# Attention forward: the two score matmuls of a step, each over its own 64 rows of the array

## The chip, the cores and the metric

The kernel runs as one program on one core of a Trainium2 chip. The engines named below are PE (TensorE, the matrix array; PEld is its weight load), DVE (VectorE), ACT (ScalarE), POOL (GpSimd) and SP (SyncE, which issues DMAs). The metric is the device time of one execution in microseconds (us); the median of repeated executions counts, and lower is better.

## The reference, cut to what matters

The whole program is the forward and the backward of one transformer block with modulated layer norms. It returns the block's output and nine gradients. The change lies in the attention of the forward pass, which reads:

```
B, S, D = 1, 2048, 512;  H = 32;  Dh = 16
q, k, v = heads of (h @ wqkv)                     # h: modulated layer norm of x
scores  = einsum('bhqd,bhkd->bhqk', q, k) * Dh ** -0.5
p       = softmax(scores, axis=-1)
o       = einsum('bhqk,bhkd->bhqd', p, v)
out     = o (heads side by side) @ wo
```

All inputs and outputs are bf16. For each of 32 heads there is a 2048 x 2048 matrix of scores, each score a sum over only 16 products, and each must pass through an exponential.

## The kernel before

**Layout.** Heads are kept in 8 groups of 4 (index g). For a group, the keys lie transposed in one tile KTq of 128 partitions by 2048 tokens: head j of the group has rows 32j to 32j+15, and rows 32j+16 to 32j+31 are zeros. Queries are stored in DRAM (QTq_d) in the same way. Four tiles QTm0 to QTm3 of 128 x 512 hold the queries of one head each: QTm[j] has head j in rows 32j to 32j+31 and zeros everywhere else, so that a matmul over all 128 rows of KTq and QTm[j] gives the scores of head j alone, the other heads being multiplied by zero.

**Loops.** The forward attention (`phase_fwd`, L267) runs over `order` (L313): 4 chunks of 512 queries (qc), in each 8 groups (g), in each two head pairs (jp). One such triple is a unit; there are 64. A unit has 16 steps, one for each block of 128 keys (kb), so there are 1024 steps. Before the change the pair jp consists of heads 2jp and 2jp+1 of the group. In a step

1. two score matmuls (L388, a = 0, 1) write 128 keys x 512 queries of each head to the two halves of a PSUM tile `st` (128 x 1024 fp32, two banks; the pool has two such tiles);
2. one ACT instruction (L391) takes the exponential of the whole tile and writes `pu` in bf16 to SBUF;
3. eight small matmuls (L322, in `pv`) of an earlier step multiply `pu` blocks (128 x 128, as weights) by 17 columns of Vaug (16 value columns and a column of ones, which gives the softmax denominator), and accumulate in `accbank`.

At the end of a unit DVE divides by the denominators (L329, L330), and POOL issues DMAs for what the next unit needs: two loads of 32 rows into the QTm tiles (`load_q`, L302), and every second unit a KTq tile (L309).

**Order.** PE and SP run in the order in which the program is written. Into each step the loop mixes background work: `bg` is a generator that first makes the remaining queries and keys (chunk 0, L631), and later runs the MLP and part of its backward for the chunk before (L1187 to L1254, L1296). `bg.step(rate)` takes on average 1.2 (chunk 0) or 1.14 (later) background matmuls of 512 columns for each step; L398 to L404 then put fewer or more of the small L322 matmuls in the step, so that a step with two background matmuls has fewer of them and a later one catches up. The order is fixed when the program is built and does not depend on measured times.

**Opening.** The first two units (32 steps, L348 to L362) are interleaved with the making of the first keys, queries and values (`gen_open`, L426). For them the queries come straight from the projection: `gen_fm` (L624) copies the 32-row strips of heads 0 to 3 into QTo0, QTo1, QTm2 and QTm3 (L641; strip 1 on ACT, the others on DVE). The six tiles QTo and QTm are first filled with zeros on DVE (L465, L469).

After the forward attention come the last chunk's MLP and weight gradients, then the attention backward (`attn_bwd`, L1422), then the last gradients. The change touches none of these. The backward matters here only because its score matmuls (L1568) and its dP matmuls (L1494) already contract over 64 rows, one in each half of the array.

Of the kernel before, what the change touches and what calls it, by code (L numbers as in the profile page):

```python
# [9 lines left out]
BF16 = mybir.dt.bfloat16  # L10
# [9 lines left out]
P = 128  # L20
# [15 lines left out]
class Background:  # L36
# [13 lines left out]
    def next(self):  # L50
        while self.gens:
            r = next(self.gens[0], None)
            if r is not None:
                if isinstance(r, tuple):
                    self.mark = r[0]
                    self.seen.add(r[0])
                return r
            self.gens.pop(0)
        return None
# [46 lines left out]
class K:  # L106
# [160 lines left out]
    def phase_fwd(self):  # L267
# [5 lines left out]
        tc, nc, pp = self.tc, self.nc, self.pp  # L273
# [15 lines left out]
        fw = self.open_pool("fw", bufs=1)  # L289
# [4 lines left out]
        stp = self.open_pool("fwst", bufs=2, space=PSUM)  # L294
        accp = self.open_pool("fwacc", bufs=2, space=PSUM)
        O32 = self.ra.tile([P, 4, D], F32, name="O32")
        QTm = [fw.tile([P, 512], BF16, name=f"QTm{j}") for j in range(4)]

        def load_q(qc, g, jp):
            with tc.high_priority():  # L300
                for j in (2 * jp, 2 * jp + 1):
                    nc.gpsimd.dma_start(QTm[j][32 * j:32 * j + 32, :], self.QTq_d[g, 32 * j:32 * j + 32, 512 * qc:512 * (qc + 1)])  # L302

        def load_k(qc, g):
            if qc == 0:
                return self.KT_next
            t = kp.tile([P, S], BF16, name="KTq")
            with tc.high_priority():
                nc.gpsimd.dma_start(t[:], self.KTq_d[g])  # L309
            return t  # L310
# [7 lines left out]
        def pv(w):  # L318
            (u, a, sub) = w
            (n, qc, g, jp, kb, acc, pu) = u  # L320
            h = 4 * g + 2 * jp + a
            nc.tensor.matmul(acc[:, a, sub, :], lhsT=pu[:, a, sub * P:(sub + 1) * P], rhs=Vaug[:, kb, h, :],  # L322
                             start=(kb == 0 and a == 0 and sub == 0), stop=False, skip_group_check=True)
            if kb < ST - 1 or (a, sub) != (1, 3):
                return
            st0 = 4 * qc
            for a in range(2):
                h = 4 * g + 2 * jp + a
                nc.vector.reciprocal(self.rl[:, st0:st0 + 4, h], acc[:, a, :, DH])  # L329
                nc.vector.tensor_tensor(O32[:, :, h * DH:(h + 1) * DH], acc[:, a, :, 0:DH],  # L330
                                        self.rl[:, st0:st0 + 4, h:h + 1].to_broadcast([P, 4, DH]), ALU.mult)
            if (g, jp) == (NQ - 1, 1) and qc < SC - 1:
                bg.add(self.gen_mlp(qc, self.take_o(qc, O32)))

        KT = kp.tile([P, S], BF16, name="KTq")
# [4 lines left out]
        QTo = []  # L340
# [7 lines left out]
        for i, (n, kb) in enumerate(units):  # L348
            if i == len(units) // 2:
                bg.until(1)  # L350
                load_q(*order[2])
            stt = stp.tile([P, 2, 512], F32, name="st")
            for a in range(2):
                nc.tensor.matmul(stt[:, a, :], lhsT=KT[:, kb * P:(kb + 1) * P], rhs=(QTm[2 + a] if n else QTo[a])[:],
                                 start=True, stop=True)
            pu = pup.tile([P, 2, 512], BF16, name="pu")
            nc.scalar.activation(pu[:], stt[:], ACT.Exp, scale=self.scale)
            u = (n, 0, 0, n, kb, accs[n], pu)
            next(first)
            pend.extend((u, a, sub) for a in range(2) for sub in range(4))  # L360
            while len(pend) > 24:
                pv(pend.pop(0))  # L362
# [5 lines left out]
        KT = self.KT_next  # L368
        for n, (qc, g, jp) in list(enumerate(order))[2:]:
            if (qc, g, jp) == (1, 0, 0):  # L370
                bg.drain()
                es.close()
                self.close_qkv()
                self.open_mlp()
                bg.add(self.gen_weights())
            accb = accp.tile([P, 512], F32, name="accbank")
            acc = accb[:, 0:8 * (DH + 1)].rearrange("p (a s e) -> p a s e", a=2, s=4)
            self.cur_g = g
            for kb in range(ST):
                if kb == (5 if qc == 0 and jp == 1 else 1) and n + 1 < len(order):  # L380
                    if n < 2 * NQ - 1 and jp == 1:
                        bg.until(g + 1)
                    load_q(*order[n + 1])
                    if jp == 1:
                        KTn = load_k(*order[n + 1][:2])
                stt = stp.tile([P, 2, 512], F32, name="st")
                for a in range(2):
                    nc.tensor.matmul(stt[:, a, :], lhsT=KT[:, kb * P:(kb + 1) * P], rhs=QTm[2 * jp + a][:],  # L388
                                     start=True, stop=True)
                pu = pup.tile([P, 2, 512], BF16, name="pu")  # L390
                nc.scalar.activation(pu[:], stt[:], ACT.Exp, scale=self.scale)  # L391
                u = (n, qc, g, jp, kb, acc, pu)
                now = n * ST + kb
                pend.extend((u, a, sub) for a in range(2) for sub in range(4))
                if late:
                    late.pop(0)()
                rate = 1.14 if qc else 1.2
                room = int((SPAN - 2 - bg.plan(rate)) / PVT)  # L398
                while pend:
                    age = now - max(pend[0][0][0] * ST + pend[0][0][4], 2 * ST - 2)  # L400
                    if age < 2 or (room <= 0 and age < 4):
                        break
                    pv(pend.pop(0))
                    room -= 1  # L404
                bg.step(rate)
            if jp == 1 and n + 1 < len(order):
                if n < 2 * NQ - 1:
                    bg.until(-(g + 1))
                KT = KTn
# [9 lines left out]
        while pend:  # L419
            pv(pend.pop(0))  # L420
# [5 lines left out]
    def gen_open(self, Vaug, KT, QTm, QTo, stp, bg):  # L426

        tc, nc, io = self.tc, self.nc, self.io
# [4 lines left out]
        sa_ = self.open_pool("p1a", bufs=1)  # L433
# [30 lines left out]
        nc.gpsimd.memset(Vaug[:, :, :, DH:DH + 1], 1.0)  # L464
        nc.vector.memset(QTm[0][:], 0.0)  # L465
        self.silu_c(ps)
        QTo.extend(sa_.tile([P, 512], BF16, name=f"QTo{j}") for j in range(2))
        for t in QTo + QTm[1:]:
            nc.vector.memset(t[:], 0.0)  # L469
        for t in self.wpad0 + wpads[::-1]:  # L470
# [2 lines left out]
        def warm(n):  # L473
            w = stp.tile([P, 2, 512], F32, name="st")
            for _ in range(n):
                nc.tensor.matmul(w[:, 0, :], lhsT=self.ones_b[:], rhs=QTm[0][:], start=True, stop=True)
# [47 lines left out]
        def pad0(t):  # L524
            nc.scalar.copy(self.wpad0[t][:].rearrange("p k (j e) -> p k j e", e=32)[:, :, :, 0:DH],
                           wq[:, :, t * D:t * D + 4 * DH].rearrange("p k (j d) -> p k j d", d=DH))
# [7 lines left out]
        def fm(*a, **k):  # L534
            for _ in self.gen_fm(ps, *a, **k):
                pass
# [22 lines left out]
        warm(4)  # L559
        fm(1, 0, 0, dst=KT[:, 0:512])  # L560
        pad0(0)
        fm(0, 0, 0, masked=QTo + QTm[2:])
        warm(2)
        for st in range(4, 8):
            stat(st)
# [1359 lines left out]
```

## Time and profile before

| | |
|---|---|
| median of 3 runs | 2545.73 us (2542.11 to 2547.05) |
| the profiled execution | 2545.66 us; its span 2543.9 us, granted TensorE clock 0.996 |
| opening, first to 33rd exponential | 16.7 to 64.2 us |
| the other 992 steps of the forward attention | 64.2 to 979.3 us |
| in that stretch (915.10 us): busy PE, ACT, DVE, POOL | 893.06, 912.01, 277.25, 271.06 us |

The profile is one execution taken by the hardware profiler. A line of its groups gives the source line, the engine, the operation, the tiles written and read, the shapes and the count; then the busy time in us and the mean length of one in ns; then the time for which the engine was idle just before them, and what ended it. For a matmul, `128*128` or `64*128` are the rows and columns of the array that it uses. A matmul's recorded end is modelled and includes the time in the pipeline: the next matmul may begin long before it. So for PE the distance from one start to the next says what an instruction costs, not its recorded length. Lines of the timeline are: start in us, length in us from the first start to the last end, engine, source line, operation, tiles, shape and count.

### The profile page before, as it was taken

How to read it: one execution, taken by the hardware profiler on the slowest of the kernel's cores; microseconds unless marked ns; L12 is line 12 of the kernel's file. 1: busy time of each engine (PE TensorE's matmuls, PEld its weight loads, DVE VectorE, ACT ScalarE, POOL GpSimd, SP SyncE). 2: the span in 40 equal slices, each digit the busy share in tenths (PEclk: the TensorE clock that was granted, in tenths of full speed). 3: DMA queues.
4: the chain of work that ended last, by engine and by line, in shares of the span. 5: the costliest groups of instructions: out<-in, count | busy, mean ns of one | idle time of the engine just before them, and what ended most of it. 6: DMA issues, size and time to landing. Idle time of an engine off the chain costs nothing.

```text
span 2543.9 us, 76653 instructions
## 1 busy us (share of the span) xinstructions
PE 2453.8 (96%) x30727; PEld 1201.3 (47%) x30727; DVE 1700.3 (67%) x3523; ACT 2299.9 (90%) x3757; POOL 707.1 (28%) x1265
## 2 busy tenths in 40 slices
PE   8999899999999999999999999999999999999998
PEld 4555555555555554663444444444444444443443
DVE  6222223423332343677999999999999999999957
ACT  7999999999999997436999999999999999999935
POOL 2454521220231031354222222222222222222223
PEclk9999999999999999999999999999999999999999
DMA  4588652440351053898999999999999999999996
GB/s 165 117 179 197 169 106 80 103 116 23 107 135 49 22 162 102 165 208 197 221 219 216 217 217 218 218 216 213 216 219 217 219 218 214 217 220 233 231 211 175
DMA packets 1258571, 442.07 MB, mean 174 GB/s; under 512 B 1203540, under 2 KB 1227222, under 8 KB 1258214
## 3 DMA queue, kind: packets, MB, share of 16 engines
q1 hardware_dynamic: 1219078, 336.03, 68.1%
q0 software_dynamic: 37056, 100.11, 13.2%
q8 instruction: 240, 3.93, 0.6%
q10 hardware_dynamic: 2080, 1.05, 0.1%
q14 instruction: 117, 0.96, 0.1%
HBM read 73.73 MB, written 62.40 MB: 54 GB/s over the span
## 4 chain that ended last, share of the span: by engine, by line
PE 58%; ACT 26%; DMA 8%; issue 5%; DVE 2%; POOL 1%; SPq 0%; DVEq 0%; ACTq 0%; POOLq 0%
ACT pu L391 18%; PE st L1568 15%; PE st L388 8%; PE acckv L1448 8%; PE accq L1470 7%; DMA dsT<-ds 7%; ACT pu L1571 6%; PE accbank L322 3%; PE dp L1494 2%; PE dps L1047 2%; PE pps L1234 2%; PE dp L1618 1%; PE pps L631 1%; PE dps L992 1%; PE st L1713 1%
## 5 line engine op out<-in xcount | busy, mean ns | idle before, releaser
L1498 DVE TENSOR_TENSOR ds<-dp,pu 128x512 bf16<-128x512 f32 x1920 | 1169.9, 681 | 67.9 <-PE dp L1494 46.6
L1571 ACT ACTIVATE pu<-st 128x512 bf16<-128x512 f32 x2048 | 1075.8, 626 | 49.1 <-PE st L1568 21.3
L391 ACT ACTIVATE pu<-st 128x1024 bf16<-128x1024 f32 x992 | 912.0, 1077 | 3.1 <-PE st L388 2.9
L388 PE MATMUL st<-QTm,KTq 128*128 128x512 bf16 x1984 | 587.7, 377 | 19.5 <-ACT pu L391 6.0
L322 PEld LDWEIGHTS <-pu 128*128 128x128 bf16 x8192 | 347.6, 96 | 235.7 <-issue 2.3
L322 PE MATMUL accbank<-Vaug,pu 128*128 128x17 bf16 x8192 | 357.7, 171 | 1.2 <-ACT Vaug L522 0.9
L1470 PEld LDWEIGHTS <-dsT 128*128 128x128 bf16 x8192 | 240.1, 96 | 229.4 <-issue 199.8
L1494 PE MATMUL dp<-m,q 64*128 64x512 bf16 x1024 | 344.4, 382 | 1.6 <-DVE g2w L1053 0.7
L1494 PE MATMUL dp<-m,dOTg 64*128 64x512 bf16 x1024 | 344.2, 382 | 0.1
L1568 PE MATMUL st<-m,QTg 64*128 64x512 bf16 x1024 | 322.1, 381 | 12.2 <-ACT pu L1571 7.5
L1568 PE MATMUL st<-m,q 64*128 64x512 bf16 x1024 | 321.6, 382 | 11.3 <-ACT pu L1571 6.7
L388 PEld LDWEIGHTS <-KTq 128*128 128x128 bf16 x1984 | 187.9, 96 | 176.1 <-issue 124.5
L1507 POOL TENSOR_TENSOR ds<-junk,pu 128x512 bf16<-128x512 f32 x64 | 74.1, 1157 | 412.6 <-ACT junk L1506 412.6
L302 POOL DMA_DIRECT2D QTm<-QTq_d x124 | 63.1, 511 | 341.0 <-PE st L388 319.5
L1448 PE MATMUL acckv<-ds,Qg 128*16 128x512 bf16 x1024 | 154.5, 382 | 0.0
L1448 PE MATMUL acckv<-pu,dOg 128*16 128x512 bf16 x1024 | 154.4, 382 | 0.0
L1448 PE MATMUL acckv<-pu,q 128*16 128x512 bf16 x1024 | 154.0, 381 | 0.0
L1448 PE MATMUL acckv<-ds,q 128*16 128x512 bf16 x1024 | 154.0, 381 | 0.0
L1470 PE MATMUL accq<-Kg,dsT 128*128 128x16 bf16 x4096 | 143.7, 170 | 10.3 <-DMA dsT<-ds 9.9
L1507 POOL TENSOR_TENSOR ds<-csq,pu 128x512 bf16<-128x512 f32 x64 | 73.9, 1154 | 281.5 <-ACT csq L1506 281.5
L1470 PE MATMUL accq<-q,dsT 128*128 128x16 bf16 x4096 | 144.6, 170 | 3.8 <-DMA dsT<-ds 3.6
L329 DVE RECIPROCAL rl<-accbank 128x4 f32<-128x4 f32 x128 | 22.9, 179 | 159.6 <-PE accbank L322 159.4
(383 smaller groups left out, 2980.3 us busy)
## 6 DMA issues: line engine op xcount, KB each, us to landing
KTq<-KTq_d POOLq DMA_DIRECT2D x24, 512.0 KB, 4.0
duT_d<-auT POOLq DMA_DIRECT2D x3, 1792.0 KB, 7.9
aT_d<-rT POOLq DMA_DIRECT2D x3, 1792.0 KB, 11.3
KTq_d<-KTq SPq DMA_DIRECT2D x32, 128.0 KB, 1.8
QTq_d<-ev_fm SPq DMA_DIRECT2D x32, 128.0 KB, 3.9
VTq_d<-vT POOLq DMA_DIRECT2D x4, 1024.0 KB, 6.5
dsT<-ds SPq DMA_TRANSPOSE x256, 7.2
dx<-dx_d SPq DMA_DIRECT2D x16, 256.0 KB, 5.6
```

The source lines that it names most:

```text
L302: nc.gpsimd.dma_start(QTm[j][32 * j:32 * j + 32, :], self.QTq_d[g, 32 * j:32 * j + 32, 512 * qc:512 * (qc + 1)])
L322: nc.tensor.matmul(acc[:, a, sub, :], lhsT=pu[:, a, sub * P:(sub + 1) * P], rhs=Vaug[:, kb, h, :], start=(kb == 0 and a == 0 and sub == 0) ...
L388: nc.tensor.matmul(stt[:, a, :], lhsT=KT[:, kb * P:(kb + 1) * P], rhs=QTm[2 * jp + a][:], start=True, stop=True)
L391: nc.scalar.activation(pu[:], stt[:], ACT.Exp, scale=self.scale)
L1047: nc.tensor.matmul(pt[:], lhsT=a[st], rhs=g_tm[:, st, :], start=(st == 0), stop=(st == ST - 1))
L1448: nc.tensor.matmul(acckv[r:r + DH, :], lhsT=T[n][:, ib, col:col + DH], rhs=src[:, a, :], start=(ib == 0), stop=(ib == ST - 1))
L1470: nc.tensor.matmul(accq[:, ib, a, :], lhsT=dsT[:, (i * 2 + a) * 4 + sub, :], rhs=T["K"][:, 4 * c + sub, col:col + DH], start=(c == 0 and i ...
L1494: nc.tensor.matmul(dp[:], lhsT=T["dOT"][rd, ib * P:(ib + 1) * P], rhs=masked["VT"][2 * jp + a][rd, 512 * c:512 * (c + 1)], start=True, sto ...
L1498: nc.vector.tensor_tensor(dsg[:, i, a], dp[:], pu[:, a, :], ALU.mult)
L1507: nc.gpsimd.tensor_tensor(dsg[:, i, 1], f[:], pu[:, 1, :], ALU.mult)
L1568: nc.tensor.matmul(stt[:], lhsT=T["QT"][rs, q], rhs=masked["KT"][2 * jp + a][rs, c0:c0 + 512], start=True, stop=True)
L1571: nc.scalar.activation(pu[:, a, :], stt[:], ACT.Exp, scale=self.scale)
```

## The change

The two heads of a unit are now heads jp and jp+2 of the group, which lie in different 64-row halves of KTq (head j in rows 32j to 32j+31). The two heads of a unit share one tile: QTm[jp] holds head jp in the lower half and head jp+2 in the upper half, each with zeros in the other 32 rows of its half. Each of the two score matmuls reads rows 0 to 63 or rows 64 to 127 of KTq and of QTm[jp]. The four tiles QTm become two and the two QTo become one, so that three of the zero fills on DVE are no longer issued; the copies and loads of strips remain as many as they were, with other targets. PE, ACT, POOL and SP issue the same instructions in the same order as before.

```
-        QTm = [fw.tile([P, 512], BF16, name=f"QTm{j}") for j in range(4)]
+        QTm = [fw.tile([P, 512], BF16, name=f"QTm{j}") for j in range(2)]
...
-                for j in (2 * jp, 2 * jp + 1):
-                    nc.gpsimd.dma_start(QTm[j][32 * j:32 * j + 32, :], self.QTq_d[g, 32 * j:32 * j + 32, 512 * qc:512 * (qc + 1)])
+                for j in (jp, jp + 2):
+                    nc.gpsimd.dma_start(QTm[jp][32 * j:32 * j + 32, :], self.QTq_d[g, 32 * j:32 * j + 32, 512 * qc:512 * (qc + 1)])
...
-            h = 4 * g + 2 * jp + a
+            h = 4 * g + jp + 2 * a
...
             for a in range(2):
-                nc.tensor.matmul(stt[:, a, :], lhsT=KT[:, kb * P:(kb + 1) * P], rhs=(QTm[2 + a] if n else QTo[a])[:],
+                r = slice(64 * a, 64 * a + 64)
+                nc.tensor.matmul(stt[:, a, :], lhsT=KT[r, kb * P:(kb + 1) * P], rhs=(QTm[1] if n else QTo[0])[r, :],
                                  start=True, stop=True)
...
                 for a in range(2):
-                    nc.tensor.matmul(stt[:, a, :], lhsT=KT[:, kb * P:(kb + 1) * P], rhs=QTm[2 * jp + a][:],
-                                     start=True, stop=True)
+                    r = slice(64 * a, 64 * a + 64)
+                    nc.tensor.matmul(stt[:, a, :], lhsT=KT[r, kb * P:(kb + 1) * P], rhs=QTm[jp][r, :], start=True, stop=True)
...
-        QTo.extend(sa_.tile([P, 512], BF16, name=f"QTo{j}") for j in range(2))
+        QTo.append(sa_.tile([P, 512], BF16, name="QTo"))
...
-        fm(0, 0, 0, masked=QTo + QTm[2:])
+        fm(0, 0, 0, masked=[QTo[0], QTm[1]] * 2)
```

## The prediction, made before the changed kernel ran

> **What bounds the kernel now.** First the page: the span, the engines' shares, the chain that ended last, and the groups of the forward attention.
>
> ```profile
> span 2543.9 us, 76653 instructions
> ...
> PE 2453.8 (96%) x30727; PEld 1201.3 (47%) x30727; DVE 1700.3 (67%) x3523; ACT 2299.9 (90%) x3757; POOL 707.1 (28%) x1265
> ...
> ACT pu L391 18%; PE st L1568 15%; PE st L388 8%; PE acckv L1448 8%; PE accq L1470 7%; DMA dsT<-ds 7%; ACT pu L1571 6%; PE accbank L322 3%; PE dp L1494 2%; PE dps L1047 2%; PE pps L1234 2%; PE dp L1618 1%; PE pps L631 1%; PE dps L992 1%; PE st L1713 1%
> ...
> L391 ACT ACTIVATE pu<-st 128x1024 bf16<-128x1024 f32 x992 | 912.0, 1077 | 3.1 <-PE st L388 2.9
> L388 PE MATMUL st<-QTm,KTq 128*128 128x512 bf16 x1984 | 587.7, 377 | 19.5 <-ACT pu L391 6.0
> ```
>
> PE and ACT both look full, and ACT sits idle for 3.1 us before its 992 exponentials, so at first sight nothing is to be had from PE. But the chain runs through both: exponentials (18%) and score matmuls (8%) in turn. So I went to the steady stretch in the busy times by window, and there to the starts of single instructions in the timeline.
>
> ```profile
> 64.20:979.30 915.10, 893.06 (x11003) 500.55 (x11000) 277.25 (x805) 912.01 (x993) 271.06 (x465) 1.00 0.46 111
> ```
>
> The 992 steps take 915.1 us, 922 ns each. PE in the timeline at 700 us:
>
> ```profile
> 700.37 0.38 PE L1296 MATMUL pps<-wogaT,dxT 128*128 128x512 bf16 x1
> ...
> 700.63 0.59 PE L388 MATMUL st<-QTm,KTq 128*128 128x512 bf16 x2
> ...
> 701.06 0.37 PE L322 MATMUL accbank<-Vaug,pu 128*128 128x17 bf16 x9
> ...
> 701.29 0.38 PE L1234 MATMUL pps<-W1mT,auT 128*128 128x512 bf16 x1
> ```
>
> Two score matmuls hold PE for 0.43 us (2 x 215 ns from start to start), the small ones 25 ns each, a background matmul 215 ns. But from the one at 700.37 to the next score matmul it is 0.26 us: PE waited some 45 ns, for ACT. From all starts in the trace, a step in this state is a loop over two steps, since `st` has two buffers: an exponential is recorded for 1088 ns; 51 ns after its end the first score matmul of two steps later starts; 215 ns later the second; that one is recorded for 377 ns; 101 ns after its end the exponential on it starts. 1088 + 51 + 215 + 377 + 101 = 1832 ns for two steps, 916 for one. Of the 991 distances between starts of these exponentials 747 are 914 to 922 ns: **the latency of this loop sets the step, neither engine's work**. ACT's own pace is the smallest distance, 904 ns; 182 are there, in runs of up to six after each delay, as the loop catches up. The exponentials overlap, so ACT shows no idle time.
>
> **The change part by part.**
>
> *Scores side by side.* What two 64-row matmuls in different halves cost is in the backward of the same trace, PE alone:
>
> ```profile
> 1701.82 0.38 PE L1568 MATMUL st<-m,QTg 64*128 64x512 bf16 x1
> 1701.82 0.38 PE L1494 MATMUL dp<-m,dOTg 64*128 64x512 bf16 x1
> 1702.13 0.56 PE L1470 MATMUL accq<-Kg,dsT 128*128 128x16 bf16 x16
> 1702.62 0.39 PE L1568 MATMUL st<-m,QTg 64*128 64x512 bf16 x1
> ...
> 1703.73 0.38 PE L1448 MATMUL acckv<-pu,dOg 128*16 128x512 bf16 x2
> 1704.04 0.39 PE L1568 MATMUL st<-m,QTg 64*128 64x512 bf16 x1
> ```
>
> The pair starts together (median 4 ns apart over 1792 pairs) and each is recorded for some 385 ns. But each change of the row count costs: from the pair to the first 128-row L1470 it is 305 ns (median of 452), 90 over the 215 of the stream; from a 512-column L1448 to the pair 311 ns (422), 96 over; from the last 16-column L1470 to the pair 101 ns (339), 76 over 25. The forward enters the pair once a step and leaves it once.
>
> Loop: 1088 + 51 + 4 + 385 + 101 = 1629, with the 96 of entry behind the wait 1725, both under 2 x 904 = 1808. So ACT's own pace takes over, with 83 to 179 ns of slack for each two steps.
>
> PE: the pair held it for 430 ns; now 4 + 305 + 96 = 405. The other matmuls of a step are 353 ns in the mean (counted at 25 and 215 ns), 455 in the heaviest 64 steps (those from 64 us on), plus 17 ns for their own waits; the remaining 122 are PE's wait for ACT (430 + 353 + 17 + 122 = 922). After: 405 + 353 + 17 = 775 in the mean, 867 in the heaviest stretch, both under 904. So PE gains only 25 ns a step; what counts is the 211 ns taken off the loop.
>
> What is late next is ACT alone: 991 x 904 = 895.9 us against 913.1 measured for these distances (the sum is over 904 by some 18 in all, first to last). By kind: the 747 at 914 to 922 and the few up to 930 give 9.9 us, all gone. 29 at 930 to 1000 are over by 1.6: steps with two background matmuls, which the slack now covers. 23 over 1000 are over by 6.6: with 179 ns of each covered (1808 - 1629) 3.7 go and 2.9 stay, most of it one step at 317 us (2.78 us) that waits for a transposing DMA. 9.9 + 1.6 + 3.7 = **15.2 us.**
>
> *Opening.* The 32 steps to 64.2 us take 47.5 us. About twenty are paced by PE (1.5 us: four 512-column matmuls, the small ones, two scores): 25 ns each, with a little where ACT waits on a pair, 0.6 us; 0.1 to 1.6 possible, since in other steps the pair's latency counts.
>
> *Three fills fewer.* They are 0.27 us each and stand ahead of the first statistics on DVE:
>
> ```profile
> 5.29 0.82 DVE L469 MEMSET QTm<- 128x256 uint32 x3
> 6.03 1.22 DVE L486 BATCH_NORM_STATS2 stats<-rT 128x6 f32<-128x512 bf16 x2
> ```
>
> The input that the statistics read landed at 5.08 us, so they move up by 0.8. The chain behind (rstd on POOL, normalization, transposes at 11.18, first score at 16.0) follows until the transposes meet their own predecessors on PE, free at 10.47: 0.7 us. At nothing if the second weight load comes late.
>
> *Copies and loads.* Same number, same places. The first pair now needs two DVE copies (end 16.26 by their lengths) where it needed one and an ACT copy (16.28): nothing. Loads into QTm are issued by POOL with the same predecessors; a tile is written while the other unit's is read, and over ten steps (9 us) remain: nothing. POOL's 319 us of waiting before them is for the score matmuls of the unit before and delays nobody. No wait is added elsewhere; one on PE changes from ACT to DVE in the opening.
>
> *After the forward* nothing changes and the background is counted in steps, so the gain stays. Its DMAs get 18 ns a step less of cover: ten steps, 0.2 us a wait, a few waits: under 1 us, not counted and inside the range.
>
> Sum: 15.2 + 0.6 + 0.7 = 16.5 us. 2545.66 - 16.5 = **2529.2 us**. The profiled execution is 0.07 us from the median of the runs shown, so the same number stands for it.
>
> [...] The 90 and 96 ns above are what this trace charges for a change of row count. [...]
>
> **Rivals.**
>
> *ACT doesn't hold 904.* The runs at 904 are six long at most, always behind a delay. If with both banks written at once it holds 910, 6 us of the gain go: 2535. If 917 is its own pace, only delays and the opening gain: 2541. Against: in the backward, where pairs write two banks at once, the 512-wide exponentials keep their smallest distance of 477 ns in a quarter of all cases, and (1024 + x) and (512 + x) columns at one rate fit 904 and 477.
>
> *Changes of mode make PE the bound: slower.* [...] A median step reaches 922 at 261 ns of change. For it: the weights of the next small matmul are loaded during the stream today, and the pair may stop that. Against: L1470 has the same 128 x 128 weights behind such a pair, at 305 ns.
>
> *The pair doesn't overlap.* Both halves come from one KTq and one QTm tile and feed one `st`; in the backward the four tiles differ. Then 222 ns apart, as two matmuls in the same half are there (L1494 to L1568): the loop is 1847 ns and a median step on PE 222 + 305 + 96 + 425 + 17 = 1065. 496 x 143 = 71 us: 2615. Against: rows and banks are split as there.
>
> **How the numbers follow.** Forecast 0.84; ACT between 904 and 917: 0.10; PE the bound: 0.04; no overlap: 0.02. Forecast's own range: the most is 18.2 + 1.6 + 0.8 = 20.6 (2525), the least, with no early start and the delays over 1000 kept, 16.5 - 0.7 - 3.7 = 12.1 (2534). Runs of one kernel lie 2.5 us either way. Range 2523 to 2538: it takes in the 910 case and leaves out the two slower rivals and ACT at 917. About 0.2% is what a measurement of this kernel tells from no change, 5 us: faster than 2540.6 is the forecast and most of ACT's case: 0.91; within 0.03; slower 0.06.
>
> **What would show it.** Starts of L391's exponentials (L392 then) 904 apart nearly throughout, their 992 in some 898 to 900 us; the two score matmuls starting within 20 ns, 64*128; 305 ns from them to the small ones; PE waiting for ACT before nearly every pair; the chain's score share falling far below 8%; first score near 15.3 us. Wrong if distances of 910 to 917 remain with PE ahead (ACT's pace), if pairs are 215 apart, or if the distance from pair to small matmuls is over 350 ns and ACT idles.

## The result, and the profile after

The changed kernel is slower: 2559.78 us median (2557.51 to 2565.97, 4 runs) beside 2543.92 us of before (2536.98 to 2547.05, 4 runs), ratio 1.0074, 95% interval 1.0051 to 1.0096. Measured once more (e9 below), the ratio was 1.0043, interval 1.0028 to 1.0059. The forecast was 2529.2 us.

The page of the changed kernel: span, engines, the row of the granted clock in 40 slices, the chain, and the two groups of the forward (their lines are now L392 and L390):

```profile
span 2564.2 us, 76651 instructions
...
PE 2474.7 (97%) x30727; PEld 1126.6 (44%) x30727; DVE 1701.1 (66%) x3520; ACT 2301.8 (90%) x3757; POOL 707.3 (28%) x1265
...
PEclk9989689989998999999999999999999999999999
...
PE 46%; ACT 36%; DMA 8%; issue 6%; DVE 2%; SPq 1%; POOL 1%; ACTq 0%; DVEq 0%; POOLq 0%
...
L392 ACT ACTIVATE pu<-st 128x1024 bf16<-128x1024 f32 x992 | 914.3, 1199 | 13.2 <-PE st L390 12.2
L390 PE MATMUL st<-QTm,KTq 64*128 64x512 bf16 x1984 | 417.3, 410 | 12.5 <-ACT pu L392 12.0
```

Two things to see. The clock row of before is 9 in all 40 slices; here a 6 and four 8s stand among the first 13. And the exponentials are now recorded for 1199 ns in the mean, not 1077, although their work is the same.

The times by window, columns as before (the granted clock is the third number from the end), first for 6.9 us before one of the slow places, 6.9 us in it and 6.2 us after it, and in the last line for all 992 steps:

```profile
212.00:218.90 6.90, 6.05 (x85) 3.28 (x83) 2.19 (x9) 6.85 (x9) 4.59 (x8) 1.00 0.60 143
218.90:225.80 6.90, 6.89 (x61) 2.45 (x60) 0.81 (x3) 5.90 (x7) 5.47 (x12) 0.51 1.04 179
225.80:232.00 6.20, 6.20 (x79) 2.73 (x78) 1.34 (x2) 6.20 (x8) 1.93 (x3) 1.00 0.85 190
62.60:990.20 927.60, 913.47 (x11003) 427.58 (x11001) 278.98 (x805) 914.38 (x993) 271.67 (x465) 0.92 0.46 109
```

For 6.8 us **TensorE ran at half its clock** (0.51 granted in the second line, 1.00 in the first and third). In PE's timeline the steps inside that place look like this, first without background work, then with it, then after the clock is back:

```profile
217.96 0.39 PE L390 MATMUL st<-QTm,KTq 64*128 64x512 bf16 x2
218.28 0.18 PE L322 MATMUL accbank<-Vaug,pu 128*128 128x17 bf16 x1
218.88 0.60 PE L390 MATMUL st<-QTm,KTq 64*128 64x512 bf16 x2 [0.41 <-ACT pu L392]
...
221.76 0.61 PE L390 MATMUL st<-QTm,KTq 64*128 64x512 bf16 x2
222.30 0.20 PE L322 MATMUL accbank<-Vaug,pu 128*128 128x17 bf16 x1
222.35 1.01 PE L632 MATMUL pps<-xm1T,wpad 128*128 128x512 bf16 x2
223.29 0.60 PE L390 MATMUL st<-QTm,KTq 64*128 64x512 bf16 x2
223.83 0.20 PE L322 MATMUL accbank<-Vaug,pu 128*128 128x17 bf16 x1
223.88 1.01 PE L632 MATMUL pps<-xm1T,wpad 128*128 128x512 bf16 x2
...
225.99 0.39 PE L390 MATMUL st<-QTm,KTq 64*128 64x512 bf16 x2
```

Before the drop PE waits 0.41 us for ACT in a step (218.88): nothing is left to do there but the pair and the small matmuls. At half clock that still fits: the exponentials that start at 218.82, 219.74 and 220.66 end 916 to 918 ns after the one before. But when the background work returns at 222, a step lasts 1.53 us (221.76 to 223.29), since at half clock streams of 512 columns take 427 ns from start to start (L1619 from 2437.97 us on, same trace) and not 215, until the clock is back at 225.8.

Where the time went, from the profiled executions (2543.9 and 2564.2 us):

| | before | after | difference |
|---|---|---|---|
| first exponential at | 16.7 us | 15.9 us | -0.8 |
| 33rd exponential at | 64.2 | 62.6 | -1.6 in all |
| the 992 steps, first start to last end | 915.1 | 927.5 | +12.4 |
| of that, delays over 916.6 ns a step, in the steps that no half-clock spell touches after | 2.7 | 1.9 | -0.8 |
| of that, the same in the 151 steps that a spell touches after (12 spells, 139.9 us) | 3.0 | 16.2 | +13.2 |
| after the last exponential | 1564.6 | 1574.0 | +9.4 |

So the half-clock spells add 13.2 us. The last row is not the change's: from 1200 to 2400 us the two traces stay some 12 to 13 us apart, and the rest comes in the last 150 us, where DMAs are waited for. In e9, the same kernel again, that part took 1559.6 us, and over all kernels below 1555 to 1568.

### The profile page after: what moved, and what is told of

Same layout as the page of the kernel before. It is cut to its first block, busy times and chain, and to the rows that moved or that the text cites. A ratio compares the mean times of both kernels' runs of the same rounds, so it can differ in the third digit from the quotient of the medians.

```text
span 2564.2 us, 76651 instructions
## 1 busy us (share of the span) xinstructions
PE 2474.7 (97%) x30727; PEld 1126.6 (44%) x30727; DVE 1701.1 (66%) x3520; ACT 2301.8 (90%) x3757; POOL 707.3 (28%) x1265
## 3 DMA queue, kind: packets, MB, share of 16 engines
q0 software_dynamic: 37056, 100.11, 13.2%
## 4 chain that ended last, share of the span: by engine, by line
PE 46%; ACT 36%; DMA 8%; issue 6%; DVE 2%; SPq 1%; POOL 1%; ACTq 0%; DVEq 0%; POOLq 0%
ACT pu L392 27%; PE st L1569 15%; PE acckv L1449 8%; ACT pu L1572 7%; PE accq L1471 7%; DMA dsT<-ds 6%; PE st L390 3%; PE dp L1495 2%; PE dps L1048 2%; PE accbank L322 2%; SPq L1697 1%; PE st L1528 1%; PE dps L993 1%; PE st L1714 1%; PE dp L1619 1%
## 5 line engine op out<-in xcount | busy, mean ns | idle before, releaser
L392 ACT ACTIVATE pu<-st 128x1024 bf16<-128x1024 f32 x992 | 914.3, 1199 | 13.2 <-PE st L390 12.2
L390 PE MATMUL st<-QTm,KTq 64*128 64x512 bf16 x1984 | 417.3, 410 | 12.5 <-ACT pu L392 12.0
L322 PEld LDWEIGHTS <-pu 128*128 128x128 bf16 x8192 | 278.2, 97 | 259.5 <-issue 254.3
L322 PE MATMUL accbank<-Vaug,pu 128*128 128x17 bf16 x8192 | 371.8, 173 | 1.3 <-ACT Vaug L523 0.9
L1569 PE MATMUL st<-m,QTg 64*128 64x512 bf16 x1024 | 322.4, 381 | 12.4 <-ACT pu L1572 7.5
L390 PEld LDWEIGHTS <-KTq 64*128 64x128 bf16 x1984 | 131.6, 94 | 245.7 <-issue 238.3
```

The lines of the kernel that those rows point to most:

```text
L390: nc.tensor.matmul(stt[:, a, :], lhsT=KT[r, kb * P:(kb + 1) * P], rhs=QTm[jp][r, :], start=True, stop=True)
L1569: nc.tensor.matmul(stt[:], lhsT=T["QT"][rs, q], rhs=masked["KT"][2 * jp + a][rs, c0:c0 + 512], start=True, stop=True)
```

## The experiments

Two theories stood against each other, beside what I had recorded. **Clock:** the pair leaves PE with too little to do in the 10 stretches of 8 to 36 steps in which no background matmul is taken (165 steps without one in all); the clock is halved there, and the loss is what follows. (Ten of the 12 spells begin in these stretches. The other two, at 89 and 315 us, begin behind steps whose background matmuls have one column each; e8 comes back to them.) **PE load:** changing the row count twice a step costs more than it saves. A third question was ACT's own pace: 904 ns, as recorded, or 917. For each kernel the profile also gave the number of half-clock spells in the forward and the length of its 992 steps (before: none, 915.1 us; changed kernel: 12, 927.5 us); these two come from one profiled execution each, the ratios from all runs.

**e1, the pair issued twice where there is no background** (138 such steps, and 25 others behind one):

```
+                for a in range(0, 0 if bg.did else 2):   # bg.did: the step before took background work
+                    r = slice(64 * a, 64 * a + 64)
+                    nc.tensor.matmul(stt[:, a, :512], lhsT=KT[r, ...], rhs=QTm[jp][r, :512], start=True, stop=True)
```

> The changed kernel, but where the step before took no background matmul (138 of the 165 steps without any) the two 64-row score matmuls are issued a second time with the same result: more PE work, only where PE has little. Theory (clock): the loss is the 12 half-clock spells of the changed kernel, one behind each of its stretches of steps without background, where PE streams for less than about 0.35 of the time. Then no spell is left in the forward, the clock is back at 0.996, and what is left is the gain: opening 1.6 us and delays 3.8 us, so some 5 us below before (ratio 0.997 to 0.999). Rival (PE load: changing the row count costs more than the two streams side by side save): added PE work can't help, ratio to before 1.006 or more. My recorded theory that ACT's own pace is 904 ns: with the clock back, 16 us below before (0.9935); if the pace is 917, exponentials still end 917 apart.

Measured: ratio 0.9992 (0.9980 to 1.0003), 2 spells, 916.9 us; clock row:

```profile
PEclk9999999999999999999999999999999999999999
```

None of the 2 spells is in a stretch without background: they stand at 89 and 311 us, behind the one-column matmuls. More work on PE took the loss away: the PE load theory falls. The gain to 904 did not come either.

**e2, only the new choice of heads**: four masked tiles as before, 128 rows.

```
-                for j in (2 * jp, 2 * jp + 1):
+                for j in (jp, jp + 2):
...
-            h = 4 * g + 2 * jp + a
+            h = 4 * g + jp + 2 * a
```

> The kernel before with only the new choice of heads (jp and jp+2 of the group in a unit), each in a masked tile of its own, scores over all 128 rows. Theory (clock): same time as before within noise (0.998 to 1.002), no half-clock spell in the forward. Rival (the pairing of heads, not the rows, costs: other columns of O, other strips to load): slower by the changed kernel's 0.6%.

Measured: 1.0006 (0.9991 to 1.0022), 1 spell of 3.4 us behind a wait of 1.7 us for a DMA (none was expected), 916.6 us. The pairing costs nothing.

**e3 and e4, the rows chosen by step**: e2 with `r = slice(64 * a, 64 * a + 64) if bg.did else slice(0, P)` in e3, `if not bg.did` in e4.

> As e2, but 64-row scores (one half of the array each, tiles of their own) in the opening and in steps that follow a step with a background matmul; 128 rows in the others. Theory (clock): activity stays over the limit in the stretches without background, no spell, and the loaded steps have the shorter pair: some 5 us below before (0.997 to 0.999). Rival (PE load): the loaded steps are where changing the row count would hurt, so as slow as the changed kernel or slower (1.006 or more). If ACT's own pace were 904 ns: 0.9945; with 917, exponentials still end 917 apart.

> The reverse of e3: 64-row scores only in steps that follow a step without a background matmul (165 or fewer of 1024), 128 rows in all others and in the opening. Theory (clock): the half-clock spells are back, about 12 in the forward, and the time is that of the changed kernel without its gains: 12 to 20 us over before (1.005 to 1.008), clock about 0.97. Rival (PE load): PE has time to spare in those steps, so no difference from before (0.999 to 1.001).

Measured: e3 0.9982 (0.9966 to 0.9997), 2 spells (none was expected: one is behind the one-column matmuls at 314 us, one behind a load of QTm that landed late), 918.6 us in its profile, 6 us of it waiting for that load. e4 1.0058 (1.0042 to 1.0075), 11 spells, 932.7 us; its clock row:

```profile
PEclk9999788999998999999999999999999999999999
```

So the 64-row pairs do harm where PE has nothing else to do, and none that shows where it is loaded.

**e5, doses**: the changed kernel, and in the same steps as e1 one more matmul, the first n columns of the second head only (`range(1, ...)`, `[:, a, :n]`).

> The changed kernel, with one more matmul of 64 columns in each step that follows a step without background: the second score matmul's first 64 columns again, same result, one half of the array. A step without background streams 213 ns (pair) + 8 x 7 ns = 270 of 917 ns, 0.295; this adds 27 ns: 0.32. Clock theory with a limit near 0.33 to 0.35: most of the 12 half-clock spells stay, ratio to before near 1.005. If the clock went by any matmul being issued, not by the time streamed, the spells would go.

> The same with 128 columns: 0.353 of the time streamed, at the limit; some spells go, between 1.000 and 1.005.

> The same with 256 columns: 0.41 of the time, over the limit: at most three spells left (those behind waits for a DMA), ratio 0.997 to 1.000, the forward some 12 us shorter than the changed kernel's.

> The same with 512 columns: 0.53 of the time streamed, but the added matmul is in one half of the rows only. If the clock counts time streamed, as at 256: no more than three spells, ratio 0.997 to 1.000. If it counted the share of the array that works, a half-array matmul would count half: (213 + 57 + 107) of 917 = 0.41, which is over the limit too, so this one bounds the effect from above and tells only whether more work ever costs time: the loop stays under two ACT steps, so it should not.

| n | ratio to before | spells | 992 steps | streaming, of 917 ns | counted by rows |
|---|---|---|---|---|---|
| 0 (e9) | 1.0043 (1.0028 to 1.0059) | 11 | 927.9 us | 0.295 | 0.295 |
| 64 | 1.0049 (1.0033 to 1.0065) | 11 | 928.2 | 0.32 | 0.31 |
| 128 | 1.0054 (1.0035 to 1.0074) | 12 | 934.2 | 0.35 | 0.32 |
| 256 | 1.0087 (1.0064 to 1.0110) | 11 | 940.4 | 0.41 | 0.35 |
| 512 | 1.0022 (1.0005 to 1.0039) | 3 | 923.9 | 0.53 | 0.41 |

My expectation for 256 failed: with PE streaming 0.41 of the time the clock still fell, and the kernel was slower than without the added matmul: the steps that touch a spell are over by 28.5 us (16.3 in e9) for the same 133 us of half clock. That the added matmul, also issued at half clock, makes these steps longer is the likely reason; no run tests it alone. Either the limit is higher, or a 64-row matmul counts as half a one (last column: 213 + 57 + half of the added stream, by 917).

**e6, 256 columns of both heads**: as long a stream as 256 above, on both halves of the rows.

> The changed kernel; in steps that follow a step without background the first 256 columns of both score matmuls are issued again, one in each half of the rows. Streams side by side, so a step without background streams as long as with 256 columns in one half alone (0.41 of 917 ns), which did not hold the clock; but counted by rows (a 64-row matmul as one half) it is 0.41 against 0.35. Theory (the clock counts the share of the array that works, limit near 0.365 by the windows of all profiles so far): at most three half-clock spells, ratio 0.997 to 1.002. Rival (it counts time streamed, limit over 0.42): 11 or 12 spells, ratio 1.005 to 1.009 as with 256 in one half.

Measured: 0.9995 (0.9981 to 1.0009), 4 spells (three were expected at most), 921.2 us. The same streaming time on all rows holds the clock in most places where half the rows did not: two of the 4 spells are behind one-column matmuls, and two in the stretches, where 256 columns in one half left ten. The windows of the two forwards, 256 in one half and then in both; the granted clock is third from the end:

```profile
62.70:1003.00 940.30, 929.57 (x11165) 424.58 (x11164) 276.01 (x805) 921.10 (x993) 271.28 (x465) 0.93 0.43 108
```

```profile
62.60:983.80 921.20, 881.50 (x11226) 427.70 (x11327) 283.68 (x805) 912.76 (x993) 271.69 (x465) 0.98 0.47 110
```

The changes of the granted clock lie on a grid: in the changed kernel's trace all 35 stand whole multiples of 3.4133 us apart, to within 5 ns. With 512 columns counted as 213 ns (half of the 427 at half clock; 215 from start to start at full clock), fewer in proportion, times rows / 128, 80 of the 81 drops in the forwards of all 14 profiles follow a grid window with about 0.37 of the array at work or less (the 12 of the changed kernel: 0.275 to 0.346), and of some 3400 windows at full clock that no drop followed 9 were below 0.37. Counted as time in which PE streams, whatever the rows, the best limit puts some 20 windows on the wrong side, not 10. The sum of all columns, whatever the rows, is out: by it the changed pair would count as much as the two matmuls before. The count was chosen after most of these runs; e6 alone tested it beforehand. Before the change no such window is under 0.42 (the lowest: 0.429, at 316 us).

**e7, the kernel before with a longer loop** in steps without background: the second score matmul's first 128 columns again, all rows.

> The kernel before; in steps that follow a step without background (163) the first 128 columns of the second score matmul are issued again, all rows. PE has time to spare there, and the loop of two steps gets 53 ns longer: 1832 becomes 1885. My recorded theory (the loop's latency, with an exponential of 1088 ns in it, sets the step): those steps take 943 ns, the forward is 4 us longer. New theory (ACT's own pace is 917 ns; the 1088 ns contain some 71 ns of waiting inside ACT, since an exponential after a delay is recorded for 1017): the loop needs 1017 + 51 + 215 + 53 + 377 + 101 = 1814, under 2 x 917, so exponentials still end 917 ns apart in these steps and are recorded for some 1035 ns instead of 1088.

Measured: 1.0000 (0.9984 to 1.0016), no spell. In the inner 108 steps of the stretches exponentials end 916.7 ns apart, as in before, and are recorded for 1034 ns (median) instead of 1088. The loop had slack, and ACT's own pace is 917.

**e8, the pair twice in exactly the steps without background** (144 in stretches of three or more).

> As e1 (both score matmuls issued twice, 512 columns), but exactly in the steps without background that come in stretches (144 steps), the first of a stretch included, and in no step with background. Clock theory: no half-clock spell but for one behind the DMA wait at 305 to 320 us; the forward's 992 steps take 909.3 us (992 x 916.6 ns) plus 2 to 5 us; ratio 0.996 to 0.9985. With the opening's 1.6 us this is the most that the change's shorter pair can give if ACT's pace is 917.

Measured: 0.9995 (0.9984 to 1.0007), 1 spell, 915.2 us, 2.8 us of delays at full clock and 3.0 behind the spell; clock row:

```profile
PEclk9999999999999999999999999999999999999999
```

The spell stands at 307 us as expected, but its cause is not the wait for a DMA that the expectation names. PE is recorded busy nearly all the time before it, and waits for nothing: the background matmuls of these steps (L1138) have one column each, so that hardly more than the pair is streamed. By the count above 0.31 of the array worked in the window before the drop. (One of the 9 windows without a drop, in e1, lies in the same steps, at 0.31 too.) One such group of matmuls, then the windows before and in the spell:

```profile
305.04 0.34 PE L1138 MATMUL pps<-sbT_b,w 128*128 128x1 bf16 x8
303.40:306.80 3.40, 3.35 (x69) 2.37 (x70) 1.99 (x6) 3.40 (x5) 1.58 (x2) 1.00 0.14 43
306.90:317.00 10.10, 10.10 (x126) 4.14 (x123) 1.80 (x5) 8.07 (x9) 8.13 (x6) 0.50 0.82 139
```

The 992 steps are no shorter than before (915.1 us): 2.9 us of delays went, and the spell brought 3.0. What e8 gains, its last exponential 1.4 us earlier than before's, is there at the 33rd exponential already (1.5 us). Of all kernels e3 alone has an interval below 1.

**e9, the changed kernel again**, for the part after the forward.

> The changed kernel once more, unaltered: its first profiled execution was the slowest of its four, and its part after the forward was 9 us longer than that of before, which the theory (clock in the forward) does not explain. If that part is spread between executions, this profile shows the forward's last exponential some 11 to 14 us later than before again, with 11 to 13 half-clock spells, and a part after it between 1555 and 1568 us, as in the other kernels; ratio to before 1.0045 to 1.006. If the change slows the later part too, that part is over 1570 us again and the ratio is 1.0075 or more.

Measured: 1.0043 (just under the range expected), 11 spells, last exponential 11.4 us after before's, 1559.6 us behind it. So the later part is as long as in the other kernels. The first measurement's 15.9 us are some 5 more than its forward lost (10.9); that these too come from the later part is likely, but only one of its four runs has a trace.

## Why the prediction was wrong

*That the forward is a loop of ACT and PE, and PE's own work not the bound: half right.* What I called the loop's latency contained its own answer. The 1088 ns of an exponential are 1017 of work, the shortest record (1017 to 1026 behind delays), and 71 that I read as waiting inside ACT: the record of an exponential begins before the one ahead of it has ended, by 173 ns in the median, and by 103 where it is 1017 long. The two lengths follow from a pace of 917: two steps of ACT are 1834 ns, the loop with 1017 in it is 1017 + 51 + 215 + 377 + 101 = 1761 before and 1017 + 51 + 4 + 385 + 101 = 1558 after, so 73 and 276 ns are left for waiting, and exponentials should be recorded for up to 1090 and 1293 ns. The longest are 1093 and 1292.

*"ACT's own pace is the smallest distance, 904 ns": this step failed first.* I now read it as the distance at which ACT accepts instructions until it has run ahead as far as the loop lets it: in the changed kernel starts 904 to 910 ns apart rose from 182 to 403, but the ends lie 917 apart in the median of both kernels (955 of 991 between 908 and 924 before, 942 after). The lines that show it are the two records, before and after, of the same instruction:

```profile
L391 ACT ACTIVATE pu<-st x992: 1017/1088/1093, 64.2 to 978.2; 128x1024 bf16<-128x1024 f32 x199
```

```profile
L392 ACT ACTIVATE pu<-st x992: 1017/1252/1292, 62.6 to 988.9; 128x1024 bf16<-128x1024 f32 x199
```

(Minimum, median and maximum in ns.) The median length grew by 164 ns while the pace stayed at 917: by that reading a queue, not work. Of the 15.2 us for the steps, 9.9 were never there. I had this as a rival, at 2541, some 5 us under before. That it would have been right without the clock isn't shown: e1, e3 and e8, which lose little to the clock, have medians 1.7, 2.9 and 0 us under before's in the same rounds.

*The delays, 5.3 us: right in kind, the size open.* Of 5.7 us before, 2.7 lie in steps that stay at full clock in the changed kernel; 1.9 of them are left. The other 3.0 lie in steps that a spell touches, where the two can't be told apart. (The 3.8 in e1's expectation is 5.7 less 1.9, and so too much.) In e8, 2.8 are left at full clock.

*Opening 0.6 and three fills 0.7: near.* 0.8 and 0.8 us.

*PE's cost of the pair: near.* In the changed kernel at full clock the two start 6 ns apart, from the second to the small matmuls it is 319 ns (305 forecast), from a background matmul into the pair 308 where PE doesn't wait for ACT (311):

```profile
690.62 0.39 PE L390 MATMUL st<-QTm,KTq 64*128 64x512 bf16 x2
690.94 0.39 PE L322 MATMUL accbank<-Vaug,pu 128*128 128x17 bf16 x9
691.19 0.38 PE L1235 MATMUL pps<-W1mT,auT 128*128 128x512 bf16 x1
```

So the changes of row count did not make PE the bound: they cost 104 and 93 ns over the 215 of a stream, 197 together, where the rival with PE as the bound needs 261. That rival named the right direction, slower, but by luck: its mechanism was wrong as well.

*"So PE gains only 25 ns a step": the step that was missing stands behind this one.* I counted how long PE is held and asked only whether it is too long, not whether it becomes too short; the sum has no term for the clock, and the spells cost 13.2 us. In a stretch without background the array worked 427 + 57 of 917 ns, 0.53, before; the pair makes it 213 + 57, 0.295. The granted clock was in the rows I read, always 1.00 in the forward, so I took it for given, though the same trace has half-clock spells outside the forward, at 1077 and 2320 us among others (granted 0.51 and 0.50). No long wait of PE stands ahead of the spells either: the longest in the windows before them is 0.41 us, and the clock falls all the same.

*Slips in the working that change no conclusion.* By the prediction's own prices the other matmuls of a step are 415 ns in the mean, not 353, so PE waited 60 and not 122 ns, and holds 837 after; in a median step they are 440, not the 425 that the rival without overlap counts; 405 + 455 + 17 is 877, not 867. All are under 904. The loop gets shorter by 203 ns (1832 to 1629), not 211; the measured distances sum to 914.0 us, not 913.1; the rival without overlap ends at 2617, not 2615.

What stays open: the limit's value is read off windows and not set by a dedicated run; 9 windows below it brought no drop, and in e5 with 512 columns the clock fell behind a window at 0.39 (377 us).

## What to carry to other kernels

Before you shorten the work of an engine that isn't the bound, look at the stretches where it has least to do: here work taken from TensorE there cost the clock in 10 of 12 spells, and the bill, 13.2 us for all 12, came when work returned. Read an engine's pace from the ends of its instructions, not from starts or recorded lengths, when these overlap (ACT here: 917 ns by ends, 904 by the closest starts, 1017 to 1293 by lengths). Where packed matmuls are wanted, use them in loaded steps and leave the idle ones as they are (e3, which gained 0.2% here; e4, the reverse, lost 0.6%).

## What the runs showed of the hardware

- The granted clock fell to 0.5 behind single windows of 3.41 us: 80 of 81 drops in the forwards of the 14 profiles follow one with about 0.37 of the array at work or less, rows counted; 9 windows below 0.37 brought no drop. In the changed kernel PE's longest idle gap in these windows was 0.41 us; spells lasted 3.4 to 34 us.
- In e8 the clock fell behind 3.4 us with PE recorded busy for 3.35, on matmuls of one column beside the 64-row pair.
- 256 added columns in one half of the rows left 11 spells (e5), in both halves 4 (e6). With a 64-row matmul counted as half of one, some 10 windows of the 14 profiles lie on the wrong side of the best limit; with streaming time alone, some 20.
- 256 columns in one half made the forward 12.5 us longer than none (940.4 in e5 to 927.9 in e9).
- ACT's exponential over 128 x 1024 fp32 from PSUM to bf16 ends 917 ns after the one before (median, before and after the change), starts as little as 904 ns after it, and is recorded for 1017 to 1293 ns.
